# The 64 left-over tokens of the last odd pair: x read with 4 as the outermost dimension and placed on other partitions, f in four loads

## The chip, the cores and the metric

The kernel runs on one core of a Trainium2 chip. The metric is the device time of one execution in microseconds (us). Three runs of the kernel before gave 197.34, 197.69 and 197.92 us; the median is 197.69 us.

## What is computed

The reference chains two layers. The first is a gated recurrence over a batch of 4 sequences of 5056 tokens with 256 channels; the second is a mixture of experts with soft slots (8 experts of 4 slots each) over all 20224 tokens.

```python
sig = 1.0 / (1.0 + np.exp(-f_logit))
f = lower_bound + (1.0 - lower_bound) * sig
for t in range(S):
    h = f[:, t] * h + (1.0 - f[:, t]) * x[:, t]       # y[:, t] = h
logits = y @ phi                                      # 32 columns, one a slot
d = softmax of logits over all tokens;  slot_input = d.T @ y
slot_out[e] = relu(slot_input[e] @ w1[e]) @ w2[e]     # 8 experts, F = 1024
out = softmax of logits over the 32 slots @ slot_out
```

Nothing of the output can be written before the last token has been read and all eight experts have run, because the slots sum over all tokens. The inputs x and f_logit are 20.7 MB each, the weights 16.8 MB in float32 (8.4 MB as they are kept, in bf16), and the output is 20.7 MB.

## The kernel before, in words

**Tiles.** Each sequence is cut into groups of 512 tokens (G, 128 partitions of R = 4 tokens); a *unit* n is one group of one sequence, and `n_unit` is 40. Units are handled in pairs that share one tile of f (`f_t`) and one of x (`x_t`), each with three buffers (pool `ld`). There are ten groups a sequence; the ninth, called `odd` (units 32 to 35), has only 448 tokens that the tenth does not cover: 3 tokens on each of 128 partitions (R3 = 3) and L = 64 left-over tokens. The 64 left-over tokens of two sequences together fill the 128 partitions of row R3 of the pair's tile, so that the even unit's tile has four rows and the odd unit's tile three.

**Loads.** `load` (lines 210 to 231) is called six units ahead. Every load of x and f is issued by SP, in order, f first and then x. A pair of `odd` takes three loads a tensor: the left-over tokens of both sequences (line 222, 128 KB, one packet of 1 KB a partition) and then 384 KB for each of the two sequences (line 226). SP uses eight completion semaphores in turn; a load that takes a semaphore waits until the load eight places before it has landed on all engines of the DMA, and a load that takes over a buffer also waits for the last reader of that buffer (ACT for f, POOL for x). The weights are loaded by POOL, in order with its other work (`load_w`, lines 135 to 147), at the units listed in `W_AT`; thirteen of the sixteen weight matrices are issued from 103.8 us on, after the last input load (100.5 us), and the last expert's second matrix is cut into four loads.

**Order of the work.** The order on each engine is written out by hand. For a unit: ACT takes the sigmoid (`gate`, line 241), POOL multiplies it with x (`enter`, line 252), TensorE (PE) turns both to channels (`s_to_channels`, `u_to_channels`), ACT makes the decay (lines 301 and 308), VectorE (DVE) runs the scan along time (line 319), PE turns the result back to tokens (line 332), and the logits, their exponentials and the slot sums follow. For the units of `odd`, `to_channels` (lines 254 to 265) writes the left-over row with one transpose whose second operand is a view of the identity, `sides`: it sends partition 2t + u to token t of sequence u. Three ordinary transposes do the other rows.

**End.** After the last unit, the expert layer works through the weights as they land (lines 605 to 759). The last expert's product gives `slot_out` (line 750), then 48 us of output writes follow (lines 772 to 861).

Of the kernel before, what the change touches and what calls it, by code (L numbers as in the profile page):

```python
# [18 lines left out]
def kernel(  # L19
# [10 lines left out]
    nc = tc.nc  # L30
    B, S, D = x.shape
# [4 lines left out]
    P = 128  # L36
# [9 lines left out]
    def first(g):  # L46
        return g * G if g < n_grp - 1 else S - G

    def used(g):
        return first(g + 1) - first(g) if g < n_grp - 1 else G  # L50
# [5 lines left out]
    R3 = used(odd) // P  # L56
    L = used(odd) - P * R3
    assert 2 * L == P

    wide_r = 4 * R  # L60
    n_blk = (S // (P * wide_r))
# [6 lines left out]
    ident_f = consts.tile([P, P], F32, name="ident_f")  # L68
# [99 lines left out]
    with tc.tile_pool(name="sp2", bufs=3) as sp2, \  # L168
# [24 lines left out]
        def long(n):  # L193
            return 2 * B <= n < n_unit - 2 * B

        def place(n):
            if long(n):
                t, j = divmod(n, 2 * B)
                return 2 * t + j % 2, j // 2
            return divmod(n, B)  # L200
# [4 lines left out]
        def tokens(src, n, k):  # L205
            g, b = divmod(n, B)
            v = src[ds(b, k), ds(first(g), G)]
            return v.rearrange("b (p r) d -> p b r d", r=R)

        def load(n, k=2):  # L210
            for src, dst, tag in ((f_logit, fs, "f_t"), (x, xs, "x_t")):
                if n % 2 == 0:
                    dst[n // 2] = ld.tile([P, 2, R, D], F32, name=tag, tag=tag)
                t = dst[n // 2]
                if long(n):
                    g, b = place(n)
                    nc.sync.dma_start(
                        out=t.rearrange("p u r d -> p (u r) d"),
                        in_=src[b, ds(first(g), 2 * G)].rearrange("(p r) d -> p r d", r=2 * R))
                elif n // B == odd:  # L220
                    b, t0 = n % B, first(odd)
                    nc.sync.dma_start(
                        out=t[:, 0, R3],
                        in_=src[ds(b, 2), ds(t0 + P * R3, L)].rearrange("b t d -> t b d"))
                    for m in range(2):
                        nc.sync.dma_start(
                            out=t[:, m, ds(0, R3)],
                            in_=src[b + m, ds(t0, P * R3)].rearrange("(p r) d -> p r d", r=R3))
                else:
                    for m in range(n, n + k):  # L230
                        nc.sync.dma_start(out=t[:, ds(m % 2, 1)], in_=tokens(src, m, 1))
# [22 lines left out]
        def to_channels(n, ps, t, rest):  # L254
            t = t.bitcast(F32)
            if n // B == odd:
                flat = ps.rearrange("c p r -> c (p r)")
                sides = ident_f.rearrange("p (t u) -> p u t", u=2)
                v = flat[:, ds(0, P * R3)].rearrange("c (p r) -> c p r", r=R3)
                k = P * R3 - n % 2 * L  # L260
                nc.tensor.matmul(flat[:, ds(k, P)], rest.bitcast(F32), sides,
                                 is_transpose=True, start=True, stop=True)
                for r in range(R3):
                    nc.tensor.transpose(v[:, :, r], t[:, r], ident_f)
                return
            for r in range(R):
                nc.tensor.transpose(ps[:, :, r], t[:, r], ident_f)  # L267
# [7 lines left out]
        def s_to_channels(n):  # L275
            if n % 2 == 0:
                pss[n // 2] = psp.tile([P, 2, P, R], F32, name="sp", tag="sp")
            to_channels(n, pss[n // 2][:, n % 2], sts[n // 2][:, n % 2],
                        sts[n // 2][:, 0, R3])

        def u_to_channels(n):
            ps = psu.tile([P, P, R], F32, name="up", tag="up")
            if long(n):
                half_to_channels(n, ps, lambda r: uts[n - n % 2 + r // R][:, r % R])
            else:
                to_channels(n, ps, uts[n], uts[n - n % 2][:, R3])
            psus[n] = ps.rearrange("c p r -> c (p r)").bitcast(BF16).rearrange(
                "c (t o) -> c t o", o=DC)
# [179 lines left out]
        for n in range(SINGLE):  # L468
            load(n, 1)
# [15 lines left out]
        for n in range(n_unit):  # L485
            if n < SINGLE - 2:
# [9 lines left out]
                if n % 2 == 0:  # L496
                    unit(load, n + AHEAD)
                unit(enter, n + 3)
                rep_constants(n)
            else:  # L500
                end = n >= n_unit - 6
                if n % 2 == 0:
                    unit(load, n + AHEAD)
                    if n == SINGLE - 2:
                        to_tokens(n - 1)
                        keep_tokens(n - 1)
                    if not end and n >= SETTLED:
                        unit(gate, n + 4)
                else:
                    unit(decay, n + 1)  # L510
                    if n < SETTLED:
                        gate(n + 3)
                    if n == n_unit - 5:
                        gate(n + 3)
                        exps(odd - 1)
# [89 lines left out]
    with tc.tile_pool(name="ew", bufs=1) as ew, \  # L605
# [36 lines left out]
        for q in range(E // Q):  # L642
# [4 lines left out]
            if q == 0:  # L647
                nc.tensor.matmul(cs_ps, rep2, cs1, start=True, stop=True)
            k = Q if q == 0 else Q - 1
            s0 = q * Q * SPE  # L650
            src = ht_ps[:, :, ds(s0, SPE)]
            src = bass.AP(tensor=src.tensor, offset=src.offset,
                          ap=[list(src.ap[0]), [P, FC], [NS + SPE, k], [1, SPE]])
# [9 lines left out]
            src = ht_ps[:, :, ds((Q - 1) * NS + s0, SPE)]  # L663
# [50 lines left out]
        for i in range(len(blocks)):  # L714
            expert(Q + i)
            row_sums(i)
            if i < len(blocks) - 1:
                spin(so_ps, 3, D)
                k = ds(i * wide_r, wide_r)
# [3 lines left out]
        k = len(blocks) - 1  # L723
# [169 lines left out]
```

## Time and profile before

| what | us |
|---|---|
| median of the three runs | 197.69 |
| the profiled execution's own time | 197.27 |
| its span in the profile | 195.5 |
| first input packet | 1.7 |
| last input landed (x of units 38 and 39) | 113.8 |
| last weights landed on the first, on the last DMA engine | 140.3, 141.95 |
| `slot_out` starts | 142.94 |
| first, last output landed | 145.0, 193.5 |

Times inside the execution are counted from the start of the span; 1.8 us of the execution's own time lie outside the span. The page gives busy time by engine, a row with the DMA's busy share in 40 slices of 4.9 us, the DMA queues (q1 is SP's, q0 POOL's, q8 and q14 fetch instructions, q10 is ACT's), and the chain that ended last. Beyond the page, the trace keeps two records that this case leans on: each DMA *packet* with its queue, start, duration and size, and each load's *landing*, one entry for every DMA engine that took part. The core has 16 DMA engines, so an ordinary load leaves 16 landing entries. The entries carry no engine number.

### The profile page before, as it was taken

How to read it: one execution, taken by the hardware profiler on the slowest of the kernel's cores; microseconds unless marked ns; L12 is line 12 of the kernel's file. 1: busy time of each engine (PE TensorE's matmuls, PEld its weight loads, DVE VectorE, ACT ScalarE, POOL GpSimd, SP SyncE). 2: the span in 40 equal slices, each digit the busy share in tenths (PEclk: the TensorE clock that was granted, in tenths of full speed). 3: DMA queues.
4: the chain of work that ended last, by engine and by line, in shares of the span. 5: the costliest groups of instructions: out<-in, count | busy, mean ns of one | idle time of the engine just before them, and what ended most of it. 6: DMA issues, size and time to landing. Idle time of an engine off the chain costs nothing.

```text
span 195.5 us, 3277 instructions
## 1 busy us (share of the span) xinstructions
PE 148.4 (76%) x1202; PEld 104.3 (53%) x1202; DVE 144.4 (74%) x187; ACT 141.9 (73%) x200; POOL 101.8 (52%) x79
## 2 busy tenths in 40 slices
PE   0687599977998979899797987998888999920000
PEld 0476468675776767667585866556664334300000
DVE  2669759989699999999999999544287998920000
ACT  3588686899889999999987799434089999950000
POOL 2689578774998688874969979253030000000000
PEclk9999759996999999999999999999999555555555
DMA  6999999999999999999999999999949999999994
GB/s 212 421 417 417 438 427 419 421 427 370 371 427 426 408 333 419 424 416 335 378 420 422 252 215 214 213 215 214 164 182 417 424 431 429 426 429 429 433 433 211
DMA packets 14305, 70.75 MB, mean 362 GB/s; under 512 B 1601, under 2 KB 2882, under 8 KB 10322
## 3 DMA queue, kind: packets, MB, share of 16 engines
q1 hardware_dynamic: 11520, 62.13, 76.8%
q0 software_dynamic: 2768, 8.42, 21.7%
q8 instruction: 9, 0.15, 0.3%
q14 instruction: 6, 0.05, 0.1%
q10 hardware_dynamic: 2, 0.00, 0.0%
HBM read 58.23 MB, written 20.71 MB: 404 GB/s over the span
## 4 chain that ended last, share of the span: by engine, by line
PE 30%; DMA 20%; DVE 16%; POOL 9%; ACT 7%; issue 5%; SPq 1%; POOLq 1%; ACTq 0%; DVEq 0%
DVE h L319 12%; DMA w_t<-in_moe_w_dram 9%; PE op L828 8%; DMA x_t<-in_x_dram 7%; POOL u_t L252 7%; ACT oc L770 5%; PE hp L332 5%; PE sp L267 4%; PE up L273 4%; DMA f_t<-in_f_logit_dram 4%; DVE ht L351 3%; PE slot_ps L189 2%; PE lg L365 2%; POOL w_sb L147 2%; PE slot_ps L416 1%
## 5 line engine op out<-in xcount | busy, mean ns | idle before, releaser
L252 POOL TENSOR_TENSOR u_t<-s_t,x_t 128x1024 bf16<-128x1024 bf16 (+1 forms) x39 | 82.5, 2131 | 22.8 <-ACT s_t L241 11.9
L319 DVE TENSOR_TENSOR_SCAN h<-a,h,up 128x512 bf16<-128x512 f32 (+1 forms) x72 | 86.8, 1252 | 4.5 <-PE up L273 2.2
L241 ACT ACTIVATE s_t<-f_t 128x2048 bf16<-128x2048 f32 (+2 forms) x23 | 38.3, 1668 | 4.7 <-DMA f_t<-in_f_logit_dram 4.6
L332 PE MATMUL hp<-ident_f,h 128*128 128x128 f32 (+1 forms) x160 | 29.5, 309 | 8.0 <-DVE ht L351 6.7
L332 PEld LDWEIGHTS hp<-ident_f,h 128*128 128x128 f32 (+1 forms) x160 | 23.5, 207 | 19.1 <-DVE ht L351 12.7
L267 PE MATMUL sp<-ident_f,s_t 128*128 128x128 f32 x144 | 22.1, 299 | 6.7 <-ACT s_t L241 4.4
L301 ACT ACTIVATE a<-sp,lbs 128x1024 f32<-128x1024 bf16 x24 | 25.4, 1114 | 1.1 <-PE sp L267 1.0
L770 ACT ACTIVATE oc<-op,rrow 128x256 f32<-128x256 f32 x62 | 24.2, 525 | 0.1
L828 PE MATMUL op<-slot_bd,etall 64*128 64x512 bf16 x62 | 22.5, 570 | 0.7 <-POOL slot_bd L759 0.4
L267 PEld LDWEIGHTS sp<-ident_f,s_t 128*128 128x128 f32 x144 | 18.2, 155 | 8.5 <-ACT s_t L241 4.9
L308 ACT ACTIVATE a<-sp,lbs 128x512 f32<-128x512 bf16 (+2 forms) x22 | 17.8, 857 | 4.7 <-PE sp L267 4.4
L766 DVE TENSOR_TENSOR oc<-op,rrow 128x512 f32<-128x512 f32 x31 | 19.8, 683 | 1.6 <-PE op L828 1.6
L273 PE MATMUL up<-ident_f,u_t 64*128 64x64 f32 x192 | 17.7, 231 | 1.8 <-POOL u_t L252 1.8
L189 PE MATMUL slot_ps<-rep,ident_f 128*128 128x256 f32 x52 | 17.5, 432 | 0.0
L273 PEld LDWEIGHTS up<-ident_f,u_t 64*128 64x128 f32 x192 | 14.1, 139 | 5.6 <-POOL u_t L252 2.1
L828 PEld LDWEIGHTS <-etall 64*128 64x128 bf16 x62 | 9.1, 153 | 13.4 <-issue 8.2
L351 ACT COPY ht<-hp 128x512 f32<-128x512 f32 (+1 forms) x20 | 11.7, 583 | 5.5 <-PE hp L332 5.3
L351 DVE COPY ht<-hp 128x512 f32<-128x512 f32 (+1 forms) x20 | 13.4, 669 | 1.4 <-PE hp L332 1.4
L319 DVE TENSOR_TENSOR_SCAN h<-a,up 128x512 bf16<-128x512 f32 x8 | 9.3, 1208 | 2.6 <-ACT a L308 1.7
L365 PE MATMUL lg<-h,phi 128*32 128x512 bf16 (+1 forms) x80 | 9.8, 412 | 0.3 <-ACT et L389 0.2
L267 PE MATMUL up<-ident_f,u_t 128*128 128x128 f32 x48 | 9.4, 327 | 0.7 <-POOL u_t L252 0.7
L189 PEld LDWEIGHTS slot_ps<-rep,ident_f 128*128 128x128 f32 x52 | 8.5, 199 | 1.8 <-issue 0.8
(132 smaller groups left out, 144.9 us busy)
## 6 DMA issues: line engine op xcount, KB each, us to landing
f_t<-in_f_logit_dram SPq DMA_DIRECT2D x12, 1024.0 KB, 12.0
x_t<-in_x_dram SPq DMA_DIRECT2D x12, 1024.0 KB, 11.5
out_dram<-oc SPq DMA_DIRECT2D x6, 2048.0 KB, 13.7
w_sb<-in_moe_w_dram POOLq DMA_DIRECT2D x14, 512.0 KB, 10.2
f_t<-in_f_logit_dram SPq DMA_DIRECT2D x12, 512.0 KB, 8.4
x_t<-in_x_dram SPq DMA_DIRECT2D x12, 512.0 KB, 9.9
out_dram<-oc SPq DMA_DIRECT2D x4, 896.0 KB, 5.7
out_dram<-ob SPq DMA_DIRECT2D x1, 2048.0 KB, 9.2
```

The lines of the kernel that those rows point to most:

```text
L189: nc.tensor.matmul(slot_bank[:, 1], ident_f, wide_rep, start=False, stop=False, skip_group_check=True)
L241: nc.scalar.activation(s_t, f_t, ACT.Sigmoid, scale=-1.0)
L252: nc.gpsimd.tensor_tensor(uts[n][:, :r], s_t[:, :r], x_t[:, :r], ALU.mult)
L267: nc.tensor.transpose(ps[:, :, r], t[:, r], ident_f)
L273: nc.tensor.transpose(v[:, :, r], t(r)[k].bitcast(F32), ident_f[k, k])
L301: nc.scalar.activation(a, sp[:, :, :, :, o], ACT.Identity, scale=nomlb[:, ds(o, 1)], bias=1.0)
L319: nc.vector.tensor_tensor_scan(h[:, :T, o], decays[n // 2, o][:, n % 2, :T], up[:, :T, o], hs[number(g - 1, b)][:, ds(used(g - 1) - 1, 1), ...
L332: nc.tensor.transpose(hp[:n_p, r], hw[:, :n_p, r], ident_f)
L351: copy(hts[g][:n_p, b].rearrange("p r d -> p (r d)").bitcast(F32), hps.pop(n)[:n_p].rearrange("p r c -> p (r c)"))
L766: nc.vector.tensor_tensor(ob, op, scale.broadcast_to(list(ob.shape)), ALU.mult)
L770: nc.scalar.activation(ob[:, i], op[:, i], ACT.Copy, scale=scale[:, i])
L828: nc.tensor.matmul(op.rearrange("p u d -> p (u d)"), ew[:, :, r], slot_bd[ds(j * 2 * NS, 2 * NS)].rearrange("s u d -> s (u d)"), start=Tru ...
```

## The change

The first odd pair (units 32 and 33) is loaded as before. For the last odd pair (units 34 and 35) the left-over rows stand on other partitions: token 4a + c of sequence u goes to partition 32c + 2a + u, where it was 2t + u. The x rows are read with two loads, one for each sequence, of 64 KB each; the DRAM side is walked with c (size 4) outermost, the SBUF side is every second partition. The f rows are read with four loads of 32 KB, one for each c, each into 32 neighbouring partitions, walked with a (size 16) outermost. The view of the identity that sorts the rows back is changed to match. SP issues 84 DMAs instead of 80; no instruction of another engine is added, removed or moved.

```diff
+    C4 = 4
...
                 elif n // B == odd:
                     b, t0 = n % B, first(odd)
-                    nc.sync.dma_start(
-                        out=t[:, 0, R3],
-                        in_=src[ds(b, 2), ds(t0 + P * R3, L)].rearrange("b t d -> t b d"))
+                    fro = src[ds(b, 2), ds(t0 + P * R3, L)]
+                    if b == 0:
+                        nc.sync.dma_start(out=t[:, 0, R3], in_=fro.rearrange("b t d -> t b d"))
+                    elif src is x:
+                        for u in range(2):
+                            nc.sync.dma_start(
+                                out=t[:, 0, R3].rearrange("(k u) d -> u k d", u=2)[u],
+                                in_=fro[u].rearrange("(a c) d -> c a d", c=C4))
+                    else:
+                        for c in range(C4):
+                            nc.sync.dma_start(
+                                out=t[ds(c * P // C4, P // C4), 0, R3],
+                                in_=fro.rearrange("b (a c) d -> c a b d", c=C4)[c])
...
-                sides = ident_f.rearrange("p (t u) -> p u t", u=2)
+                if n % B < 2:
+                    sides = ident_f.rearrange("p (t u) -> p u t", u=2)
+                else:
+                    sides = ident_f.rearrange("p (c a u) -> p u a c", c=C4, u=2)
```

## The prediction

> **What bounds the kernel.** I read the page's DMA rows first, then the busy time by stage, then the chain of waits, and then the trace's landing and packet records.
>
> ```profile
> DMA  6999999999999999999999999999949999999994
> GB/s 212 421 417 417 438 427 419 421 427 370 371 427 426 408 333 419 424 416 335 378 420 422 252 215 214 213 215 214 164 182 417 424 431 429 426 429 429 433 433 211
> ...
> q1 hardware_dynamic: 11520, 62.13, 76.8%
> ...
> q8 instruction: 9, 0.15, 0.3%
> q14 instruction: 6, 0.05, 0.1%
> q10 hardware_dynamic: 2, 0.00, 0.0%
> ```
>
> The DMA is busy in nine tenths or more of every slice but the first, the last and the one at 142 to 147 us. The 215 GB/s from 112 us on is no idleness: the weights are read in float32 and counted as the bf16 that is written. By stage, the last columns being DMA share and GB/s:
>
> ```profile
> 96.00:98.00 2.00, 2.00 (x31) 1.20 (x30) 2.00 (x3) 1.87 (x2) 1.72 (x1) 1.00 1.05 416
> 112.00:125.00 13.00, 10.88 (x97) 8.09 (x95) 12.26 (x12) 11.50 (x17) 9.30 (x13) 1.00 1.06 214
> 125.00:142.00 17.00, 15.43 (x244) 10.25 (x243) 6.12 (x17) 4.64 (x11) 4.97 (x9) 1.00 1.01 196
> 147.00:194.00 47.00, 24.05 (x73) 10.18 (x71) 22.51 (x37) 26.49 (x70) 0.00 (x0) 0.55 0.99 419
> ```
>
> Until 142 us the DMA reads inputs and weights without a pause, and from 147 us it writes without one. What joins the two is the chain:
>
> ```profile
> 119.16 2.15 POOL w_sb L147 x4
> 121.31 18.04 DMA w_t<-in_moe_w_dram
> 139.35 0.04 issue
> 139.39 0.40 PE sum_ps L670 x8
> ```
>
> A weight load issued at 121.31 lands at 139.35 because it stands behind others. So the end is the time at which the *last of the 16 DMA engines* has moved its share, plus the 53.5 us of span that follow it.
>
> The landing records show how far the engines stand apart. The last weight load but one landed at 139.98, 139.99, 140.03, 140.35, 140.39, 140.56, 140.62, 141.09 on eight engines and between 141.25 and 141.64 on the other eight; the very last landed from 140.32 to 141.95. Nine engines are thus 1.1 to 1.7 us behind the first, and these set the end. The packet records tell why. The instruction packets of 16 KB on q8 take 0.88 to 0.98 us each, at 29.4, 50.2, 63.1, 77.6, 94.1, 108.7, 125.5 and 135.4 us; after each, one more entry of every landing stands 1.1 to 1.5 us behind. They hit a different engine each time. Before the change's place, at 96 us, five entries are 1.34 to 1.56 us behind and eleven less than 0.8; three more are hit later. An engine that has work queued never makes up its lag.
>
> The Trainium skill ("Runtime: NRT & Kernel Launch", Instruction fetch mechanics) says that instructions are refilled in blocks of 16 KiB; the packet sizes on q8 agree (9 packets, 0.15 MB), and the skill's remark that crossing a block is mostly hidden does not hold for the data loads here.
>
> **The change, part by part.**
>
> *x on fewer engines.* The 128 KB load of line 222 leaves 16 landing entries and gives each engine 8 packets of 1 KB, 46 ns each in the packet records (43 from start to start): 0.34 us an engine. The one load of this kernel whose outermost size is under 16 is ACT's `lb_row` (size 1): q10 shows one data packet and one 4-byte packet, so a single engine carried it. I take it that a load with 4 outermost uses 4 engines; the bounds are 1 engine and 16. Two loads of 64 packets on the same four engines are 32 packets each: 32 × 43 ns = 1.38 us instead of 0.34. Four engines get +1.03 us, twelve get −0.34 us.
>
> What that does to the end hangs on which four. If none of the four is among the engines that are late or will be, the end comes 0.34 us earlier. If one of them is late at 96 us (1.34 to 1.56) or is hit later, it ends at 1.57 + 1.03 = 2.60, where the last stood at 1.66: +0.94 us, or +1.03 if it is the very last. Nothing in this profile numbers the engines. Eight of sixteen had been hit by 16 KB packets before 142 us; four drawn blindly miss all eight once in 26 times. Hits that follow some pattern make a miss far likelier, so I put it near one in two.
>
> The Trainium skill ("DMA: Bandwidth & Descriptors", Rules for kernel authors, row "Use all 16 engines") says that an outermost size below 16 confines a load to at most that many engines. It speaks against this change, and by it the four loaded engines would be those of the +1.03 us. Its section on how many engines are used adds that they are the lowest-numbered; no row here shows numbers.
>
> *f in four loads.* Each has 16 outermost and 32 packets, two an engine: the same 8 packets in all, plus three completion packets of 9 ns, 0.03 us. The gate of this pair runs late enough:
>
> ```profile
> 98.96 1.70 ACT L241 ACTIVATE s_t<-f_t 128x1792 bf16<-128x1792 f32 x1
> ```
>
> f of this pair landed at 97.55, 1.4 us before.
>
> *The SP queue.* Four more DMAs take four more of the eight semaphores in turn, so that each later load waits for a smaller one.
>
> ```profile
> 88.37 1.10 SPq L226 DMA_DIRECT2D f_t<-in_f_logit_dram  x2
> 89.66 0.56 SPq L222 DMA_DIRECT2D x_t<-in_x_dram  x1
> 90.61 2.92 SPq L226 DMA_DIRECT2D x_t<-in_x_dram  x2
> 94.42 1.28 SPq L231 DMA_DIRECT2D f_t<-in_f_logit_dram  x2
> ```
>
> The second load of the x pair waited until 93.20 for a load that landed on its last engine at 93.19. With four more in the row I get these issues: second 384 KB f load 93.20 (that same landing); first 64 KB x load 94.37 (landing 94.36); second 95.37 (landing 95.36); first 384 KB x load about 95.9, when SP has finished the issue before (0.56 us by line 222). The data of a load starts 1.0 us after its issue (0.72 to 1.75 at the start of the span), so at 96.9. An engine that is not behind finishes the second f load at 96.0 and is not among the four: it stands idle for 0.9 us, and then moves its x packets. Before, it finished the first of them at 97.30; now at 97.9 if the restart costs nothing, 98.2 if the first packet takes 0.35 us more, as after the idle start of the span. So the leading engines lose 0.6 to 0.9 us, those 1.3 us behind lose nothing. That would be free if the leaders stayed leaders, but three of them are hit afterwards. The one hit at 108.7 stood 0.17 us behind and ended last at 1.66; from 0.6 to 0.9 it ends at 2.1 to 2.4: +0.4 to +0.73 us, I take +0.55. If the cover of queued work is larger than I think, this term is nothing.
>
> *Nothing else is on the path.* The permuted `sides` costs at worst a doubling of four transposes (0.11 us each on the chain), before 111 us; weights issued 112.7 to 121.3 land 10 to 18 us later, so POOL has several us in hand. `enter` of the pair starts at 101.67, its x landed at 99.79; +1.03 us on four engines makes 100.8. If that cover were gone, POOL's weight issues (103.75 on) would slip, with some 4 us of queued work before an engine noticed.
>
> ```profile
> 101.67 2.16 POOL L252 TENSOR_TENSOR u_t<-s_t,x_t 128x1024 bf16<-128x1024 bf16 x1 [1.61 <-ACT ht L351]
> 103.75 0.59 POOL L137 DMA_DIRECT2D w_sb<-in_moe_w_dram  x1
> ```
>
> **Sum.** One of the four engines is among the late ones: +0.94 us, which also covers the idle gap (other engines, not added). 197.27 + 0.94 = 198.21 for the profiled execution; the median of the three runs stands 0.42 higher, so 197.69 + 0.94 = 198.6 us.
>
> **Rivals.**
> 1. *Gap alone* (the four are never hit, but the leaders run dry at 96 us): +0.55, 198.2 us (198.0 to 198.5). For it: SP's issue is already tied to the last engine's landings. Against: 0.9 us of idleness rests on two latencies taken from elsewhere in the span.
> 2. *Lighter load on the late engines* (the other side): the four are leaders and stay so, and enough work is queued at 96 us: −0.34, 197.35 us. It decides if every late engine is among the twelve and the gap stays under 0.3 us. For it: seven engines end 1.0 us or more ahead of the last, room for the extra 1.03 us. Against: the four must be among these seven. The Trainium skill ("DMA: Bandwidth & Descriptors", Latency and other measured facts) holds that engines 7 and 15 are usually the slow ones, which would favour it; by the landings here it is nine, and a step of 1.1 to 1.5 us each.
> 3. *The load spreads anyway* over 16 engines: work per engine is as before; only SP's longer row is left, 197.7 to 198.3 us.
>
> **How the numbers follow.** Forecast 0.50, gap alone 0.28, lighter load 0.17, spread anyway 0.05. The range has to reach rival 2 on one side and +1.03 with 0.3 us of run-to-run spread on the other: 197.3 to 199.0; the forecast's own is 198.3 to 199.0. A measurement tells about 0.3% (0.6 us) from no change, so the bounds are 197.1 and 198.28. Slower: 0.45 of the forecast's 0.50 and half of the gap's = 0.59. Faster by 0.6 us needs more than the 0.34 us: 0.05. The same: 0.36.
>
> **What would show it.** The x loads' landing records: five entries each (one for the twelve idle, four for engines) if 4 engines carry them, 17 if not. The last weight load's landings: an entry at 2.6 us behind if the forecast holds, all within 1.3 if rival 2 does. Engine idleness near 96 us, and SP's issues at 95.4 to 96.3, show the gap. I would be wrong if hits by instruction packets fell otherwise after the change, or if the last weights did not set the end.

## The result, and the profile after

Four runs of the changed kernel gave 200.18 to 201.19 us, median 200.38; four of the kernel before gave 197.34 to 197.92, median 197.68. The ratio is 1.0146 (95% interval 1.0114 to 1.0177): **2.7 us slower**, outside the range that was forecast (197.3 to 199.0). The profiled execution after is the slowest of its four, 201.19 us with a span of 199.4.

First the DMA rows of the page after, against the same rows of before in the prediction:

```profile
DMA  6999999999999999999899999999929999999994
GB/s 213 417 420 421 431 431 419 426 432 322 417 419 424 379 371 419 426 412 293 274 342 337 279 276 223 215 213 214 167 84 413 424 450 421 421 421 450 444 421 214
```

From the nineteenth slice (89.7 us; a slice is 5.0 us here and 4.9 us before) to the twenty-second the GB/s are 293, 274, 342, 337, where before had 335, 378, 420, 422. Ahead of those slices the inputs stream at much the old rate, and from the twenty-fifth on the weights do (223, 215, 213). So the loss lies around the changed loads. The stage of 20 us that holds them, before and then after (last two columns DMA share and GB/s):

```profile
84.00:104.00 20.00, 18.33 (x176) 13.90 (x174) 19.52 (x19) 19.24 (x19) 15.23 (x9) 1.00 1.03 387
```

```profile
84.00:104.00 20.00, 17.51 (x169) 13.41 (x165) 19.51 (x20) 17.81 (x18) 15.67 (x10) 1.00 0.96 330
```

57 GB/s less over 20 us is 1.14 MB that had not moved. At the 420 GB/s of a full stage that is **2.7 us**. This is a figure of the profiled execution, which is 3.9 us slower than the one before; the median is 2.7 us slower, and the other executions left no trace, so that the two figures of 2.7 agree is not shown to be more than chance. The landings tell how the loss builds up. The leading engine is 0.7 us later than before at the second 384 KB f load (96.65 against 95.99), 2.1 us at the first 384 KB x load (99.42 against 97.30), 2.8 us at the second 512 KB x load behind it (106.04 against 103.23), and 3.0 us at the last weights. In steps of 2 us, after and then two of before:

```profile
94.00:96.00 2.00, 2.00 (x26) 1.47 (x26) 2.00 (x3) 2.00 (x3) 2.00 (x2) 1.00 0.98 301
96.00:98.00 2.00, 2.00 (x31) 1.46 (x24) 1.95 (x2) 1.68 (x3) 2.00 (x2) 1.00 0.75 233
98.00:100.00 2.00, 2.00 (x18) 1.86 (x16) 1.67 (x2) 1.85 (x3) 1.34 (x1) 1.00 0.92 335
100.00:102.00 2.00, 2.00 (x18) 1.75 (x17) 1.90 (x2) 2.00 (x4) 1.18 (x1) 1.00 0.90 300
102.00:104.00 2.00, 0.85 (x7) 0.45 (x5) 2.00 (x4) 0.34 (x1) 1.98 (x3) 1.00 0.93 348
104.00:106.00 2.00, 2.00 (x16) 1.87 (x16) 2.00 (x2) 0.84 (x1) 1.71 (x2) 1.00 1.02 416
```

```profile
98.00:100.00 2.00, 2.00 (x18) 1.77 (x18) 1.62 (x2) 1.52 (x2) 2.00 (x2) 1.00 1.04 425
100.00:102.00 2.00, 2.00 (x20) 1.74 (x19) 1.90 (x3) 1.99 (x3) 0.39 (x2) 1.00 1.01 412
```

A share under 1 means that DMA engines had nothing to do. It shows only a part of the loss, because a packet that takes longer than usual counts as busy; the bytes show more of it. Before, no step of 2 us from 92 to 106 us was under 1.01. PE and DVE are much as busy as before up to 102 us; it is the DMA that went hungry, and the reason stands in SP's queue:

```profile
86.12 4.61 SPq L233 DMA_DIRECT2D f_t<-in_f_logit_dram  x4
92.58 1.43 SPq L237 DMA_DIRECT2D f_t<-in_f_logit_dram  x2
94.80 1.71 SPq L228 DMA_DIRECT2D x_t<-in_x_dram  x2
96.56 0.93 SPq L237 DMA_DIRECT2D x_t<-in_x_dram  x2
97.60 0.85 SPq L242 DMA_DIRECT2D f_t<-in_f_logit_dram  x2
```

SP issued the 384 KB f loads at 92.58 and 93.68 and the 384 KB x loads at 96.56 and 97.06. Before, these four went out at 88.37, 89.14, 90.61 and 93.20. The landing records give the cause of each date. The first f load waited for the load eight places before it, whose last engine landed at 92.56; the second for one at 93.66; the x loads for the two small x loads (94.80, 95.93), which waited for 94.74 and 95.92. Until 96.56 nothing stood in the queue behind the second f load but 128 KB of x on four engines. The first engine had landed that f load at 96.65, and the first packet of the 384 KB x load starts at 97.68. This is the hole. The chain after, followed back from the last x load, says the same in one piece:

```profile
84.37 11.55 DMA x_t<-in_x_dram
95.92 0.02 issue
95.93 0.59 SPq L228
96.52 0.04 issue
96.56 0.45 SPq L237
97.01 0.04 issue
97.06 5.36 DMA x_t<-in_x_dram
102.42 0.02 issue
102.43 21.01 DMA x_t<-in_x_dram
```

An x load lands on its last engine at 95.92 and frees SP's semaphore; SP issues a small x load and then the 384 KB ones; the second of them lands at 102.42 and frees the semaphore of the last x load. That one leaves 0.5 us ahead of the next weights (102.92), where before it left 3.3 us ahead (100.46 and 103.75), shares the DMA with more of them, and lands at 123.45 instead of 113.84. POOL waits for it and issues its weights later:

```profile
119.82 2.14 POOL L263 TENSOR_TENSOR u_t<-s_t,x_t 128x1024 bf16<-128x1024 bf16 x1 [5.65 <-DMA x_t<-in_x_dram]
123.61 2.14 POOL L263 TENSOR_TENSOR u_t<-s_t,x_t 128x1024 bf16<-128x1024 bf16 x1 [1.65 <-DMA x_t<-in_x_dram]
125.69 2.17 POOL L148 DMA_DIRECT2D w_sb<-in_moe_w_dram  x4
```

That last delay cost nothing more, because the DMA still had weights queued: it read 2.1 to 2.2 MB in each 5 us from 120 us to 135 us, before and after alike.

The rest of the change did what it says. Each small x load left five landing entries: one 1.0 to 1.1 us after its issue, which I read as standing for the engines that do not take part, and four for those that do (97.47 to 97.97 for the first). The very last weight load landed 0, 0.17, 0.24 ... 1.43, 1.62 and **2.60** us behind the first engine (before: 0 ... 1.59, 1.63): one engine stands alone at the end. With the first engine 3.0 us later (143.32 instead of 140.32), the last is 4.0 us later, and that is the 3.9 us of the profiled execution. The lone engine is not the mark of the small x loads, though. Behind the hole the first 384 KB x load landed within 0.9 us on all 16 engines (99.42 to 100.30): the hole had levelled them. The second landed from 100.37 to 101.28 on fifteen and at 102.42 on one, so the late one fell behind after the hole.

### The profile page after: what moved, and what is told of

It reads as the page before. It is cut to its first block, busy times and chain, and to the rows that moved or that the text cites. A ratio compares the mean times of both kernels' runs of the same rounds, so it can differ in the third digit from the quotient of the medians.

```text
span 199.4 us, 3283 instructions
## 1 busy us (share of the span) xinstructions
PE 150.1 (75%) x1202; PEld 105.5 (53%) x1202; DVE 144.9 (73%) x187; ACT 142.3 (71%) x200; POOL 101.8 (51%) x79
## 4 chain that ended last, share of the span: by engine, by line
DMA 48%; PE 19%; POOL 9%; DVE 5%; ACT 4%; issue 2%; SPq 1%; POOLq 1%; ACTq 0%
DMA x_t<-in_x_dram 33%; PE op L842 9%; DMA w_t<-in_moe_w_dram 8%; DMA f_t<-in_f_logit_dram 7%; POOL u_t L263 7%; DVE h L333 3%; ACT oc L784 3%; PE up L287 2%; PE op L790 2%; PE hp L346 2%; PE sp L281 1%; POOL w_sb L148 1%; DVE ht L365 1%; PE slot_ps L190 1%; ACT ht L365 1%
## 5 line engine op out<-in xcount | busy, mean ns | idle before, releaser
L842 PE MATMUL op<-slot_bd,etall 64*128 64x512 bf16 x62 | 23.4, 596 | 0.4 <-POOL slot_bd L773 0.4
L379 PE MATMUL lg<-h,phi 128*32 128x512 bf16 (+1 forms) x80 | 9.0, 390 | 0.0
```

Of the source, the lines that this page charges most:

```text
L842: nc.tensor.matmul(op.rearrange("p u d -> p (u d)"), ew[:, :, r], slot_bd[ds(j * 2 * NS, 2 * NS)].rearrange("s u d -> s (u d)"), start=Tru ...
```

## The experiments

**Theory A**: SP counts landings on eight semaphores in turn, so each load waits for the one eight places before it to land on its last engine; six small loads in this row leave too little queued, and the DMA runs dry. **Theory B**: the 128 KB on four engines cost the time. **Theory C**, the forecast: one of the four engines is late anyway and ends about 1 us later. All ratios are to the kernel before, run on the same chip (medians 197.50 to 197.52 us; 197.68 for the change).

| kernel | DMAs that SP issues | median us | ratio (95% interval) | GB/s 84 to 104 us | last weights on the first engine, us | spread of the engines there, us |
|---|---|---|---|---|---|---|
| before | 80 | 197.50 to 197.52 | | 387 | 140.32 | 1.63 |
| the change | 84 | 200.38 | 1.0146 (1.0114 to 1.0177) | 330 | 143.32 | 2.60 |
| f in four | 83 | 199.86 | 1.0116 (1.0101 to 1.0131) | 354 | 142.10 | 2.47 |
| x on four engines | 81 | 198.22 | 1.0043 (1.0026 to 1.0060) | 384 | 140.36 | 2.53 |
| rows only | 84 | 200.44 | 1.0150 (1.0126 to 1.0174) | 332 | 143.46 | 2.65 |
| change with 80 loads | 80 | 198.81 | 1.0064 (1.0044 to 1.0084) | 360 | 142.09 | 1.66 |
| small loads last | 84 | 200.66 | 1.0149 (1.0128 to 1.0171) | 347 | 142.77 | 1.84 |
| f in four, first pair | 83 | 197.86 | 1.0019 (1.0008 to 1.0030) | 381 | 140.47 | 1.94 |
| x in two | 81 | 197.36 | 0.9995 (0.9986 to 1.0004) | 386 | 140.24 | 1.88 |
| before, merged | 76 | 197.19 | 0.9987 (0.9979 to 0.9996) | 387 | 140.47 | 1.62 |
| f in four by POOL | 79 | 197.21 | 0.9989 (0.9977 to 1.0002) | 379 | 141.13 | 2.21 |
| f in two, x in two | 82 | 198.84 | 1.0067 (1.0040 to 1.0095) | 366 | 141.36 | 3.17 |

The last three columns are of one profiled execution each, and this need not be one near the median: it took 201.19 us for the change and for rows only, 199.67 for small loads last, 198.25 for f in four by POOL and 199.66 for f in two, x in two. A hole shows as a late first engine; the spread shows how far the last one stands behind it.

**f in four**, in the old order of tokens:

```diff
+                        for c in range(4):
+                            nc.sync.dma_start(
+                                out=t[ds(c * P // 4, P // 4), 0, R3],
+                                in_=fro[:, ds(c * L // 4, L // 4)].rearrange("b t d -> t b d"))
```

> f of the last odd pair in four loads in the old token order, x in one load, everything on all 16 DMA engines: three more entries in SP's row, no load confined to four engines. Theory A (SP's row of eight semaphores: more and smaller loads in the row leave too little queued, so the DMA runs dry between 94 and 104 us): slower than before by 1.0 to 2.5 us. Theory B (the 128 KB on four engines are what costs): within 0.3 us of before.

Measured 2.3 us slower, with nothing on four engines. Theory B alone can't give that; A said 1.0 to 2.5. SP's own time for issuing the small loads (0.56 to 0.63 us each) is a rival that the landings settle: SP was free from 95.34 and issued the first 384 KB x load at 95.76, when the load eight places before had landed at 95.74.

**x on four engines**, f in one load:

```diff
+                        for u in range(2):
+                            nc.sync.dma_start(
+                                out=t[:, 0, R3].rearrange("(k u) d -> u k d", u=2)[u],
+                                in_=fro[u].rearrange("(a c) d -> c a d", c=4))
```

> x of the last odd pair in two loads on four engines as in the changed kernel, f in one load as before: one more entry in SP's row. The gate rows keep the old order, so the 128 left-over tokens of this pair are multiplied with other tokens' gates; the work is the same. Theory A: most of the 2.7 us is gone, between 0 and +0.8 us of before. Theory B: +2 us or more. Theory C (load on the four engines, one of which is hit by instruction packets): +0.9 to +1.1 us.

Measured 0.7 us in the medians and 0.86 in the profiled executions (198.13 against 197.27). The DMA did not run dry:

```profile
84.00:104.00 20.00, 18.20 (x174) 13.75 (x172) 19.51 (x20) 19.23 (x19) 15.35 (x9) 1.00 1.03 384
```

The last weight load's entries are 0, 0.12, 0.13, 0.37, then eleven from 1.01 to 1.68, then 2.53. The loaded engines can be followed by time. The last 1 KB packet of x starts at 97.86, and 31 steps of 43 ns before that is 96.5, so all four had begun their x packets by then. None is one of the five late engines, which landed the f load ahead at 97.69 or later. Behind the small x loads nine entries stand back instead of five: the first 384 KB x load landed at 97.25 to 97.73 on seven engines and at 98.42 to 99.34 on nine. Its last entry is 2.1 us behind, and the last entry stays 1.9 to 2.1 us behind until 135 us; after the instruction packets at 135.4 (16 KB) and 136.7 (8 KB) it is 2.53. So this is the forecast's mechanism, by its second way (an engine that is hit later), and nearly its size; that the packets fell so was luck.

**Rows only**, the changed kernel's six loads without any on four engines, in the old order of tokens:

```diff
-                                in_=fro[u].rearrange("(a c) d -> c a d", c=C4))
+                                in_=fro[u])
...
-                                in_=fro.rearrange("b (a c) d -> c a b d", c=C4)[c])
+                                in_=fro[:, ds(c * L // 4, L // 4)].rearrange("b t d -> t b d"))
```

> f in four loads and x in two as in the changed kernel, but all of them on 16 engines and in the old token order: four more entries in SP's row and nothing on four engines. Theory A: nearly all of the 2.7 us, +1.8 to +2.8 us. Theory B: within 0.3 us of before.

Measured 2.9 us slower, as much as the change itself, with the same hole in the same place:

```profile
84.00:104.00 20.00, 17.64 (x168) 13.47 (x164) 19.51 (x20) 17.93 (x18) 15.61 (x10) 1.00 0.98 332
```

Theory B is out for the 2.7 us. In this kernel, too, one engine ends 2.65 us behind, though all engines have the same bytes. As in the changed kernel it fell behind after the hole: the second 384 KB x load landed within 0.6 us on all 16 engines (100.38 to 100.97), the next load from 101.76 to 103.92.

**The change with 80 loads**: the 384 KB loads of both odd pairs merged by twos.

```diff
-                    for m in range(2):
-                        nc.sync.dma_start(
-                            out=t[:, m, ds(0, R3)],
-                            in_=src[b + m, ds(t0, P * R3)].rearrange("(p r) d -> p r d", r=R3))
+                    nc.sync.dma_start(
+                        out=t[:, :, ds(0, R3)].rearrange("p u r d -> p u (r d)"),
+                        in_=src[ds(b, 2), ds(t0, P * R3)].rearrange("b (p r) d -> p b (r d)", r=R3))
```

> the changed kernel, but the two 384 KB loads of each odd pair and tensor are one load of 768 KB: SP issues 80 DMAs again. Theory A: the DMA does not run dry, what is left is the uneven load: between -0.35 and +1.0 us of before. Theory B: +2 us or more. Theory C: +0.9 to +1.0 us and an entry 2.6 us behind in the last weights' landings.

Measured 1.3 us slower, in between. The number of loads is that of before, but the look-back of eight still falls on a late one. In SP's queue:

```profile
91.24 3.24 SPq L228 DMA_DIRECT2D x_t<-in_x_dram  x2
96.04 0.38 SPq L236 DMA_DIRECT2D x_t<-in_x_dram  x1
```

The 768 KB x load left at 96.04, when the x load eight places before it had landed on its last engine at 96.02. The leading engine landed the f load ahead at 96.48, and the 768 KB landed from 99.94: 1.9 us of transfer and 1.6 us of hole. So my expectation that 80 loads suffice was wrong; by this trace it counts which load stands eight places back, not the total. The last weights end 1.66 us apart, as before: no engine at 2.6. The hole let the loaded engines catch up: the 768 KB landed within 0.6 us on all 16.

**Small loads last**: the same 84 loads as the change, the last pair's small ones moved behind the loop that issues its 384 KB ones.

```diff
                     if b == 0:
                         nc.sync.dma_start(out=t[:, 0, R3], in_=fro.rearrange("b t d -> t b d"))
-                    elif src is x:
+                    for m in range(2):
+                        nc.sync.dma_start(
+                            out=t[:, m, ds(0, R3)],
+                            in_=src[b + m, ds(t0, P * R3)].rearrange("(p r) d -> p r d", r=R3))
+                    if b and src is x:
...
-                    else:
+                    elif b:
...
-                    for m in range(2):
-                        nc.sync.dma_start(
-                            out=t[:, m, ds(0, R3)],
-                            in_=src[b + m, ds(t0, P * R3)].rearrange("(p r) d -> p r d", r=R3))
```

> the changed kernel with the same 84 loads, but the small loads of the last odd pair stand behind its 384 KB loads instead of ahead of them. Theory A (what counts is how much is queued while SP waits for the load eight places before): the second 384 KB loads are issued 3 us earlier and at least half of the 2.7 us is gone; with one of the four engines late, +0.7 to +1.3 us of before. If the number of loads alone counts: +2.5 us or more.

Measured 3.2 us slower in the medians: a miss. (The profiled execution, 199.67 us, is the fastest of the four.) The 384 KB loads did leave earlier (f at 86.20 and 88.59, x at 94.65 and 95.59), but the hole only moved behind them:

```profile
94.65 1.27 SPq L227 DMA_DIRECT2D x_t<-in_x_dram  x2
96.89 1.58 SPq L232 DMA_DIRECT2D x_t<-in_x_dram  x2
98.57 0.87 SPq L242 DMA_DIRECT2D f_t<-in_f_logit_dram  x2
```

The small x loads waited for the landings of the two 384 KB f loads (96.88 and 97.86), and the 512 KB f loads behind them, issued at 94.42 before, came to 98.57. I had followed the row only as far as the 384 KB loads.

**f in four, first pair** instead of the last:

```diff
-                    if b == 0 or src is x:
+                    if b or src is x:
```

> the kernel before with f in four loads on 16 engines in the first odd pair instead of the last. Theory A: loads of 1 MB are still queued ahead of them, so little or nothing runs dry there, but the row of the last pair is then three places further back: 0 to +1.0 us of before. If three more loads cost their issue and fixed time wherever they stand: +2.3 us, as with the last pair.

Measured 0.4 us slower. The same three extra loads cost a sixth where 1 MB loads are queued ahead of them (issued from 78.50 on, while the 1 MB loads issued at 73 to 78 us still took until 83.5 to 88.8 us to land).

**x in two** on all 16 engines:

```diff
-                                in_=fro[u].rearrange("(a c) d -> c a d", c=4))
+                                in_=fro[u])
```

> the kernel before with x of the last odd pair in two loads on all 16 engines: one more entry in SP's row, nothing on four engines. The counterpart of the kernel with x on four engines (+0.7 us). Theory A with C: within 0.3 us of before, so that the four engines made the 0.7 us. If the extra entry made it: +0.7 us.

Measured 0.1 us faster, interval across no change. One extra load costs nothing. With the kernel above that differs from it by the four engines alone, the four engines cost 1.0043 − 0.9995, or 0.9 us (0.6 to 1.3 with the two intervals).

**Before, merged**:

> the kernel before with the two 384 KB loads of each odd pair and tensor as one of 768 KB (76 loads in all). Theory A: nothing ran dry before, so within 0.3 us of before; if fewer loads in the row are worth something by themselves, up to 0.5 us faster.

Measured 0.3 us faster (ratio 0.9987, interval up to 0.9996), with the same edit as in the change with 80 loads. It is the only version whose interval lies below no change, and the gain is small: nothing ran dry in the kernel before (387 GB/s in both), so there is little to win.

**f in four by POOL**: as in the first experiment, but with `nc.gpsimd.dma_start`.

> the kernel with f in four loads on 16 engines and x in one (+2.3 us when SP issued all of them), but the four small loads are issued by POOL, which counts them on semaphores of its own: SP's row loses one entry instead of gaining three. POOL spends about 2.2 us on the four issues while it has some idle time. Theory A (SP's row of eight): within 0.4 us of before. If four small loads cost the DMA itself that time whoever issues them: +2 us or more.

Measured 0.3 us faster, interval across no change, against 2.3 us slower when SP issued the same four loads. POOL spent the time where it had it:

```profile
95.04 2.08 POOL L227 DMA_DIRECT2D f_t<-in_f_logit_dram  x4
```

This decides for A: the four small loads cost nothing that can be measured in the DMA itself; issued by SP they cost 2.3 us, and the landing dates under f in four put that down to their places in SP's row.

**f in two, x in two**:

> f of the last odd pair in two loads and x in two, all on 16 engines: two more entries in SP's row (one more gave 0, three +2.3, four +2.9 us). Theory A: the second 384 KB f load still waits for the same landing, but two packets' worth less of the row stands ahead of it; +0.2 to +1.5 us, between one more and three more. If the cost sets in with f's loads alone: as with one more, within 0.3 us.

Measured 1.3 us slower, with runs from 197.57 to 200.31 us. One, two, three and four extra loads thus cost −0.1, 1.3, 2.3 and 2.9 us. These kernels also differ in which tensor is split, so this is no series in the number alone. In the one execution that was profiled (199.66 us) the first engine had the last weights 1.0 us later than before, and the last engine was 3.17 us behind it. The wide range would fit a DMA that runs dry in some executions and hardly in others; without more traces that is not shown.

## Why the prediction was wrong

- **What bounds the kernel: right.** The DMA's last engine sets the end. In the profiled executions the last weights landed 4.0 us later (145.93 against 141.95), and `slot_out` started 3.9 us later (146.86 against 142.94), with no other engine's work in the way.
- **x on four engines: right in mechanism, and in size partly by luck.** Run by itself, four engines took the load, and the last engine ended 2.53 us behind against 2.60 forecast; it costs 0.9 us (forecast +0.94). Up to 135 us it stood 1.9 to 2.1 us behind, and the last 0.5 us came with late instruction packets. In the changed kernel itself the hole levelled the engines, and nothing of this cost can be seen.
- **The step that failed is "the SP queue"**, the term of 0.4 to 0.73 us that was put at +0.55 and then not even added. Its mechanism was right, the waits for the load eight places before, but it measured 2.3 us with f's three extra loads alone and 2.9 us with all four and nothing on four engines. Three things in it were off:
  1. *Who stands idle.* The prediction said "those 1.3 us behind lose nothing" and counted one hole for the leading engines. Landings of the loads show all 16 engines pushed: the first 384 KB x load landed from 99.42 to 100.30, where before it landed from 97.30 to 98.88. The hole was longer than the late engines' lag, so it closed over them too.
  2. *How long a hole lasts.* I allowed 1.0 us from issue to data and up to 0.35 us for the restart. From the issue at 96.56 to the first packet it was 1.1 us, but then the first packets of 3 KB took 0.2 to 0.9 us instead of 0.121, and the load landed 2.9 us after its issue, of which its eight packets an engine are 0.95 us. So 1.9 us, not 1.35. The kernel before had this price on record: its very first load was issued at 0.72 and landed from 3.93 on, 3.2 us for 1.27 us of packets, and its first packets took 0.51 to 0.90 us, so that 0.35 us more than 0.159 was the least of them and not the rule. With 1.9 us my own reckoning has the leading engines lose about 1.45 us instead of 0.6 to 0.9 (an estimate from these rows).
  3. *How many.* I followed the look-back for four loads, with the landings of before. In the run the first 384 KB f load waited until 92.56, not 90.60, because the late engines' landings of that load came later here. So this load was already short of cover: the leading engine was 0.3 us late at it, 0.7 at the second f load, and 2.1 at the first x load. The records show what had moved: the packets of POOL's weight load, which take their turn on the same engines, began at 89.65 instead of 90.24.
- **The sum.** "Other engines, not added" was the second fault: a hole that every engine falls into moves the end by itself, whether a loaded engine is late or not. That the two do not add up the other way either is seen in rows only (2.9 us without the four engines, against 2.7 us with them): the two differ by less than their intervals. That in the hole the loaded engines have work while the others wait would fit this.
- **Rivals.** "Gap alone" named the right cause with a fifth of its size. "Lighter load on the late engines" needs both that the four are never late and that no gap opens; neither held.
- **The rest.** The gate, POOL and the permuted view of the identity cost nothing that the end shows, as forecast; rows only, with the old view, is no faster. The rule in the Trainium skill ("DMA: Bandwidth & Descriptors", Rules for kernel authors) that an outermost size below 16 confines a load to at most that many engines agrees with the four landing entries; it explains the 0.9 us of x on four engines and none of the 2.7.

Left open are two things. The first is the weaker stretch from 100 to 104 us (300 and 348 GB/s), in which the leading engine loses about 0.7 us more. Its loads had been issued 2 us or more before, at 97.60 to 98.96, and single packets of 4 KB still took 0.2 to 1.1 us instead of 0.159. No run separates a late issue from a slow restart there.

The second is the weight load. In the profiled executions of the five kernels in which SP issues more than one extra load for the last pair and the 384 KB loads stay apart, POOL issued it at 85.7 to 85.9 us, ahead of any changed load, and the last 384 KB f load of the first pair landed at 92.4 to 92.6; in the other kernels it was issued at 86.3 to 87.7, and that landing was at 90.6 to 91.6. No run moves the weight load by itself. It can't be the whole: with the landings of before the prediction had the first 384 KB x load leave at 95.9, and it left at 96.56, so at most 0.7 us of that date can come from later landings.

## What to carry to other kernels

When the DMA is the bound, count what is *queued*, not what is moved: with a fixed number of loads in flight, each small load takes the place of a large one, and the queue holds fewer bytes while the issuer waits. Walk the look-back through every load until the queue is full again, with the landing on the last engine as the date, and don't stop at the loads that were changed; here each load into a dry queue paid nearly 2 us of restart, and a hole that is longer than the lag of the late engines pushes all of them. If small loads are needed, give them another issuer or put them where large ones are queued ahead.

## What the runs showed of the hardware

- A load into an empty queue landed 2.9 us after its issue for 0.95 us of packets: 1.1 us to the first packet, and first packets of up to 0.9 us (the change, first 384 KB x load). The first load of the kernel before took 3.2 us for 1.27.
- A load on four engines leaves five landing entries, and the first came 1.0 to 1.1 us after the issue, before any of its data; I read it as the count of the absent twelve.
- In the kernel before, each 16 KB instruction packet set one more engine back by 1.1 to 1.5 us, and the lag stayed to the last weights. It went where the queue ran dry: after the hole of the change with 80 loads all 16 engines landed within 0.6 us.
